# One fixed order for all engines: a list schedule in the kernel in place of key-sorted stages with visits

## The chip, the core and the metric

The kernel runs on one core of one Trainium2 chip. Five engines work at the same time, each through its own queue of instructions: PE (TensorE, matmuls; its weight loads are a row of their own, PEld), DVE (VectorE), ACT (ScalarE), POOL (GpSimd), and SP (SyncE), which here only issues DMA transfers. They meet through semaphores. The metric is the device time of one execution in microseconds (us); 374.27 us before, the median of three runs.

## The reference, cut to what matters

A gated linear attention feeds a feed-forward layer with a convolution along the sequence. There are 4 sequences of 768 steps, 8 heads of 48, so d_model is 384; d_ff is 1024.

```python
f = 1.0 / (1.0 + np.exp(-f_logit))
for t in range(S):
    state = f[:, :, t, :, None] * state + np.einsum('bhd,bhe->bhde', k[:, :, t], v[:, :, t])
    y[:, :, t] = np.einsum('bhd,bhde->bhe', q[:, :, t], state)
...
h = np.maximum(x @ w_in, 0.0)                 # x: y with heads side by side
hp = np.concatenate([zeros, h, zeros], axis=1)
for k in range(3):
    conv_out += conv_w[k][None, None, :] * hp[:, k:k + S, :]
gate = 1.0 / (1.0 + np.exp(-conv_out))
return (h * gate @ w_out).astype(np.float32)
```

The three weight arrays come as float64, q, k, v and f_logit as float32.

## The kernel before, in words

**Tiling.** The sequence is cut into chunks of 128 steps: 6 per sequence, 24 in all, numbered n. Three chunks make half a sequence, a unit u; there are 8 units. Attention goes chunk by chunk, the feed-forward unit by unit. All of it is unrolled; nothing loops on the chip.

**Attention of a chunk.** *Gate*: two activations (Exp, Ln) turn f_logit (tile fb) into log decays; from group 3 on, three chunks at once and split into two reduced-precision parts (cgh, cgl). *Stage a*: a matmul with a triangle sums the decays into pl; ACT takes two exponentials, fi and fd; k is multiplied by fi, q by fd; the last row of fd is the chunk's decay, fetched by small matmuls into pl (L223) for the first chunks and by small DMAs (L238, L246) later. *Stage b*: four transposes each of k and q (ptk, ptq, L254), copied to kT and qT (L256). *Scores*: 16 matmuls into pa (L298), copied under a causal mask into am (L300). *Values*: py gets the old state times q (L340), then v times am (L346); ACT and DVE split it into two parts of xT (L356, L357). *State*: 16 matmuls of k with v (L313) and two DVE steps (L322, L323) give the next state. pa, py and fi have one buffer, am, kT and qT two, xT three, k four, q three. After each third chunk six DMAs inside the core gather part of xT (L362).

**Weights.** w_in comes in six tiles, w_out in eight. `split_f64` (L98) turns the two 32-bit words of each number into a high and a low float part: three ACT and up to seven DVE steps, and for tiles marked d or a in `CFG["ez"]` three matmuls on PE (pzwi, pzwo) that form the low part, copied out by DVE or ACT. The raw words lie in the buffers of g and xT for that time.

**Feed-forward.** `mm1` (L367) takes two of the eight d_ff tiles of a unit: nine matmuls each into ph (L385), Relu into hb (L388), the three taps of the convolution on ACT and DVE (L390, L396, L397), a Tanh (L399) and the gate product (L400) into g. `mm2` (L402) takes 128 steps: g is split into gh and gl (L415, L416), 24 matmuls go into po (L422), ACT copies to ob, SP stores. ph, po and the weight joins share two PSUM banks.

**What sets the order.** Each stage is put into a list with a key (L440 to L475), mostly a chunk number with an offset from CFG; the list is sorted by key and traced. What each engine then runs is not this order: the framework orders the instructions again by priority and its own timeline (`schedule_with_timeline_sim=True`, L614). `visit` (L272) ties parts of it down: from chunk 8 (`ng`) on, score, value and state matmuls get a high priority (`hp`); the first value matmul of a chunk waits for the copies of kT, qT and am of this and the next chunk; the state matmuls follow the last visited PE instruction. Two matmuls on zeros (L264) go ahead of all. Behind the list, a count checks the decays (L483 to L489) and a branch leads to a slow path that is not taken here.

Of the kernel before, what the change touches and what calls it, by code (L numbers as in the profile page):

```python
# [9 lines left out]
F32 = mybir.dt.float32  # L10
# [12 lines left out]
CFG = dict(ez="ddddddaaaavvvv", ng=8, hp=4000, tb=2, groups=[3, 3, 3, 3, 3, 3, 3, 3], sg=3, f1=2.6, g1=2.6, gv=9, gl=5.2, g=3.9, l=3.2, a=1.8, b=0.8, s=0.2, v=0.5, wil=(-2.3, -1.1), wis=(-0.7, 0.9), cw=1.3, wol=(1.3, 1.0), wos=2.1, wo=0.35, m1=0.5, m1s=0.9, m2=1.5, m2s=1.2, ek=(12, 24), ec='d', er='p', tp=0, tf=2, nw=2, gd=0, q0=2, lf=3, kpool=2, eg='d', eq='d', es='d', em='d', ew='p', xb=3, nf=6, fe='a', kb=4, qb=3, vb=4, lv=2.2, cb=1, sb=3, fi=1)  # L23

@with_exitstack
def gla_moe_kernel(ctx, tc, q_in, k_in, v_in, f_in, w_in, conv_w, w_out, out):
# [5 lines left out]
    q, k, v, f_logit = [t.rearrange("b s h d -> b h s d")[:, :, :, :D] for t in (q_in, k_in, v_in, f_in)]  # L32
# [7 lines left out]
    GC = max(groups)  # L40
    first = [sum(groups[:g]) for g in range(len(groups) + 1)]
# [12 lines left out]
    ld = fast.enter_context(tc.tile_pool(name="ld", bufs=2))  # L54
    wk = fast.enter_context(tc.tile_pool(name="wk", bufs=2))
# [21 lines left out]
    def zeroed(shape, n, name, eng):  # L77
        ts = [wk.tile(shape, F32, name=f"{name}{i}", bufs=1) for i in range(n)]
        for t in ts:
            eng.memset(t, 0.0)  # L80
        return ts

    kp_b = [wk.tile([P, H, HP], F32, name=f"kp{i}", bufs=1) for i in range(CFG["kb"])]
    qp_b = [wk.tile([P, H, HP], F32, name=f"qp{i}", bufs=1) for i in range(CFG["qb"])]
    a_b = zeroed([P, 2, NP, P], 2, "am", nc.vector)
    s_b = [wk.tile([P, NP * D + GAP], F32, name=f"st{i}", bufs=1) for i in range(2)]
# [4 lines left out]

# [6 lines left out]
    def split_f64(raw, n, hi, lo, nm, tile=0):  # L98

        pr = raw.rearrange("p (n w) -> p n w", w=2)  # L100
        lw, hw = pr[:, :, 0], pr[:, :, 1]
        r = raw.shape[0]
        ms = wk.tile([P, 2, WC], I32, tag="gl", name=f"ms{nm}")
        m, s = ms[:r, 0, :n], ms[:r, 1, :n]
        mf, sf = m.bitcast(F32), s.bitcast(F32)
        nc.scalar.activation(mf, hw.bitcast(F32), AF.Abs)
# [23 lines left out]
    raws = {}  # L130

    def raw_in(kt, i):
        if kt == 0 and ("i", i) not in raws:
            raws["i", i] = wk.tile([P, KT, 2 * WC], I32, tag="g32", name=f"wis{i}")
        return raws["i", i][:, kt]

    def raw_out(f):
        i = f // 4
        if ("o", i) not in raws:
            raws["o", i] = (wk.tile([P, 4, 2 * DM], I32, tag="g32", name=f"wos{i}") if i == 0 else  # L140
                            wk.tile([P, 4, 2 * DM], I32, tag="xT", name=f"wos{i}", bufs=CFG["xb"]))
        return raws["o", i][:, f % 4]

    def load_w_in(kt, i):
        nc.sync.dma_start(raw_in(kt, i), w_in[kt * P:(kt + 1) * P, i * WC:(i + 1) * WC].bitcast(I32))
# [473 lines left out]
```

## Time and profile before

| what | before |
|---|---|
| median of three runs | 374.27 us (371.98 to 374.36) |
| the profiled execution | 374.75 us |
| its span, first to last instruction | 373.0 us |
| mean granted TensorE clock | 0.969 |
| busy PE / PEld | 349.7 / 308.4 us |
| busy DVE / ACT / POOL | 266.0 / 236.6 / 15.0 us |
| instructions | 7517 |
| read from HBM / written | 28.37 / 4.75 MB |

Busy times are of one engine and overlap with the others. The ends of matmuls are modelled, so a busy PE need not be PE at its peak. A row of the timeline has start and length in us, engine, line, operation, output<-inputs, and in brackets the idle time before it with what ended it; neighbouring rows of one kind are merged (x3), and rows of one engine overlap a little where instructions are pipelined. A row of the chain of waits has start, length, and what the end of the kernel waited for. A row of a group has line, engine, operation, count, then busy us and mean ns of one. SPq is SP's queue, which issues transfers; PEldq is PE's queue.

### The profile page before, as it was taken

The numbers are of one execution on the slowest core, as the hardware profiler recorded it, in microseconds if no ns is written. First come the engines' busy times: TensorE is split into PE (matmuls) and PEld (weight loads), VectorE is DVE, ScalarE is ACT, GpSimd is POOL, SyncE is SP. The second block draws the span as 40 slices with busy tenths as digits, with TensorE's granted clock in tenths as the row PEclk, the third lists the DMA queues.
The fourth block names the chain that finished last, engine by engine and source line by source line (L and its number), as shares of the span: only waits on it lengthen the run. The fifth ranks groups of instructions, "written<-read, shape, count | busy, mean of one in ns | idle before, by whom it ended". The sixth has DMA issues, their size and how long they took to land.

```text
span 373.0 us, 7517 instructions
## 1 busy us (share of the span) xinstructions
PE 349.7 (94%) x2927; PEld 308.4 (83%) x2927; DVE 266.0 (71%) x443; ACT 236.6 (63%) x425; POOL 15.0 (4%) x45
## 2 busy tenths in 40 slices
PE   4788999977999998999999999999999999999993
PEld 1456677865899986899999898999999999999992
DVE  3598897989577836867768887679578766576620
ACT  3769887896957657756947664476455744566530
POOL 1110000014000000100000000000000000000000
PEclk9598999998799999999999999999999999999998
DMA  7998226324312360233321442223021000201011
GB/s 229 357 354 320 103 44 188 114 79 119 106 29 72 93 195 15 100 69 98 101 73 51 112 126 67 66 71 101 22 72 34 21 2 24 54 23 42 21 46 50
DMA packets 28854, 36.05 MB, mean 97 GB/s; under 512 B 10847, under 2 KB 20106, under 8 KB 28810
## 3 DMA queue, kind: packets, MB, share of 16 engines
q1 hardware_dynamic: 28810, 35.49, 31.3%
q8 instruction: 25, 0.41, 0.4%
q14 instruction: 19, 0.16, 0.1%
HBM read 28.37 MB, written 4.75 MB: 89 GB/s over the span
## 4 chain that ended last, share of the span: by engine, by line
PE 75%; DVE 10%; ACT 6%; DMA 4%; issue 3%; SPq 1%; ACTq 0%; DVEq 0%
PE po L422 26%; PE ph L385 23%; PE py L346 6%; PE pa L298 5%; PE py L340 3%; PE ptk L254 3%; PE py L313 2%; PE ptq L254 2%; DMA fb<-in_f_logit_dram 2%; PE pl L214 2%; DMA wis<-in_moe_w_in_dram 2%; DVE g L397 1%; PE pzwi L125 1%; ACT fb L188 1%; DVE g L396 1%
## 5 line engine op out<-in xcount | busy, mean ns | idle before, releaser
L385 PE MATMUL ph<-xT,wi 128*128 128x384 f32 x576 | 113.3, 345 | 0.8 <-ACT ob L425 0.8
L385 PEld LDWEIGHTS ph<-xT,wi 128*128 128x128 f32 x576 | 99.8, 189 | 4.5 <-issue 1.4
L422 PE MATMUL po<-wo,gh 128*128 128x384 f32 x384 | 99.8, 339 | 1.5 <-ACT hb L388 1.5
L422 PEld LDWEIGHTS po<-wo,gh 128*128 128x128 f32 x384 | 69.2, 188 | 2.7 <-ACT hb L388 1.8
L422 PE MATMUL po<-wo,gl 128*128 128x384 f32 x192 | 65.3, 340 | 0.0
L396 DVE SCALAR_TENSOR_TENSOR g<-hb,cw,g 128x384 f32<-128x384 f32 (+1 forms) x64 | 39.3, 616 | 19.8 <-ACT g L390 19.3
L388 ACT ACTIVATE hb<-ph 128x384 f32<-128x384 f32 x64 | 31.5, 492 | 30.6 <-PE ph L385 30.4
L415 ACT CAST gh<-g 128x1024 fp32r<-128x1024 f32 (+4 forms) x34 | 26.7, 803 | 27.1 <-PE po L422 21.9
L416 DVE TENSOR_TENSOR gl<-g,gh 128x1024 fp32r<-128x1024 f32 (+4 forms) x34 | 30.5, 909 | 17.9 <-ACT gh L415 15.9
L399 ACT ACTIVATE g<-g 128x768 f32<-128x768 f32 (+1 forms) x32 | 27.1, 846 | 25.1 <-DVE g L397 25.1
L400 DVE SCALAR_TENSOR_TENSOR g<-g,hb 128x768 f32<-128x768 f32 (+1 forms) x32 | 30.7, 960 | 15.4 <-ACT g L399 15.2
L397 DVE SCALAR_TENSOR_TENSOR g<-hb,cw,g 128x384 f32<-128x384 f32 (+1 forms) x64 | 39.5, 619 | 2.5
L390 ACT ACTIVATE g<-hb,cw 128x384 f32<-128x384 f32 (+1 forms) x64 | 39.6, 620 | 1.9
L422 PEld LDWEIGHTS po<-wo,gl 128*128 128x128 f32 x192 | 36.0, 188 | 0.8 <-issue 0.5
L300 DVE COPY_PREDICATED am<-mask,pa 128x1024 f32<-128x1024 uint8 x24 | 31.7, 1320 | 1.1 <-PE pa L298 1.1
L346 PE MATMUL py<-am,v 128*48 128x128 f32 (+1 forms) x384 | 28.9, 291 | 2.9 <-DVE xT L357 1.7
L298 PE MATMUL pa<-qT,kT 48*128 48x128 f32 x384 | 29.9, 286 | 1.6 <-ACT qT L256 1.1
L298 PEld LDWEIGHTS pa<-qT,kT 48*128 48x128 f32 x384 | 24.3, 187 | 6.9 <-issue 1.8
L346 PEld LDWEIGHTS py<-am,v 128*48 128x48 f32 (+1 forms) x384 | 22.2, 136 | 8.6 <-issue 4.6
L357 DVE TENSOR_TENSOR xT<-py,xT 112x512 fp32r<-112x512 f32 x24 | 16.5, 689 | 4.2 <-ACT xT L356 4.2
L356 ACT CAST xT<-py 112x512 fp32r<-112x512 f32 x24 | 14.0, 584 | 7.8 <-PE py L346 7.8
L378 POOL COPY hb<-hb 128x4 f32<-128x4 f32 x16 | 9.9, 619 | 186.1 <-DVE g L400 186.1
(106 smaller groups left out, 400.5 us busy)
## 6 DMA issues: line engine op xcount, KB each, us to landing
kp<-in_k_dram SPq DMA_DIRECT2D x24, 256.0 KB
qp<-in_q_dram SPq DMA_DIRECT2D x24, 256.0 KB
fb<-in_f_logit_dram SPq DMA_DIRECT2D x24, 192.0 KB
v<-in_v_dram SPq DMA_DIRECT2D x24, 192.0 KB
out_dram<-ob SPq DMA_DIRECT2D x24, 192.0 KB
wis<-in_moe_w_in_dram SPq DMA_DIRECT2D x6, 512.0 KB
wos<-in_moe_w_out_dram SPq DMA_DIRECT2D x8, 384.0 KB
xT<-xT SPq DMA_DIRECT2D x48, 48.0 KB
```

The source lines that it names most:

```text
L298: nc.tensor.matmul(pa[:, j, p, :], kT[r, p, :], qT[r, p, :], start=True, stop=True)
L300: ready.setdefault(n, []).append(nc.vector.copy_predicated(am, mask, pa).ins)
L346: nc.tensor.matmul(py[HP * o:HP * o + w, j, p // 2, :], lhs, am[:, j, p, :], start=c == 0 and p < 2, stop=(p >= 2))
L385: nc.tensor.matmul(ph, wi[:, t, wl, f * P:(f + 1) * P], xts[b, hf][:, t, xl, :], start=(i == 0), stop=(i == 3 * KT - 1))
L388: nc.scalar.activation(hb[:, 2:HS + 2], ph, AF.Relu, scale=0.5)
L390: nc.scalar.activation(cv, hb[:, 1:n + 1], AF.Copy, scale=cw[:, 1, f:f + 1])
L396: nc.vector.scalar_tensor_tensor(cv, hb[:, 2:n + 2], cw[:, 2, f:f + 1], cv, ALU.mult, ALU.add)
L397: nc.vector.scalar_tensor_tensor(cv, hb[:, 0:n], cw[:, 0, f:f + 1], cv, ALU.mult, ALU.add)
L399: nc.scalar.activation(cv, cv, AF.Tanh)
L400: nc.vector.scalar_tensor_tensor(cv, cv, 1.0, h_b[:, fp:fp + 2, 1:n + 1], ALU.add, ALU.mult)
L416: nc.vector.tensor_tensor(lo, g[:, f:f + k], hi.bitcast(F32), ALU.subtract)
L422: nc.tensor.matmul(po, g[:, f, :], wo[:, f, wl, :], start=(i == 0), stop=(i == 3 * NF - 1))
```

## The change

The keyed stages, `visit` and the helper functions go. Every step becomes an item (`Op`) of a `Plan`: which engine, how many ns, what to issue, a key, which items it needs (`need`), which buffer it takes from a ring (`take`) and which buffers it uses (`use`). An item is about one ACT, DVE or POOL instruction or DMA, or one group of matmuls: the transposes of k, those of q, the 16 scores, the carry (old state times q), the 16 values, the state matmuls, nine ph matmuls, sixteen po matmuls on gh and eight on gl, the three joins of a weight tile.

`Plan.order()` is a list schedule, run in Python while the kernel is built. It keeps a clock. Whenever an engine is free, it takes, of the items whose needs are done and whose buffers are free, the one with the smallest key; rings hand out buffers in the order of keys. An item ends after its ns, and is seen by others after a further latency for its engine. From matmuls of the r kind (reduced precision) to the f kind 95 ns are added, for an ACT table change 1283. A load lands by a pipe that moves 340 bytes per ns, 1500 ns after its issue at the earliest, plus 700; at most eight are in flight. `trace()` then issues all items in the order of planned starts under `manual_schedule()`, so that this is the order on each engine.

Keys are a chunk number with new offsets from CFG: per unit for mm1 and mm2 (`m1`, `m2`), per weight tile for the splits (`w1s`, `w2s`). Further edits in it:

- Weight loads of the first half of w_in have the key -5.73, conv_w -5.15, f of chunk n n - 3.97 (n + 27.31 from group 3 on), k and q n - 1.96, v n + 10.34.
- Copies to kT and qT, and the last copy of a weight split, go to ACT or DVE, whichever the plan has free first.
- 11 weight tiles are joined on PE and 3 on DVE (before 10 and 4).
- The first two k products move from POOL to DVE. The two warm-up matmuls on zeros are gone. The state needs no tmp tile.
- mm2's matmuls go first over gh, then over gl, where before each tile of d_ff took both. The last 128 steps are no longer split into quarters.
- The count of decays is traced behind the whole plan.

The arithmetic, the matmuls' shapes and the number of buffers of each kind stay; the raw weight words may now lie in two of xT's buffers and in both of g's, whichever is free first.

```diff
+    LAT = dict(PE=210, ACT=70, DVE=70, POOL=100, SP=60)
...
+            for e in free:
+                if free[e] > now + 1e-6:
+                    continue
+                if e == "SP" and len(dma) >= 8 and dma[-8] > now + 1e-6:
+                    continue
+                for o in sorted(ready[e], key=lambda o: o.key):
...
+                    for r, i in o.take:
+                        if fifo[r][head[r]] is not o:
+                            ok = False
+                            break
+                        b = next((b for b in self.rings[r] if not (b[1] & taken)), None)
...
+                ns = o.engs[e]
+                if e == "PE":
+                    if mode == "r" and o.mode == "f":
+                        ns += 95
+                    mode = o.mode
...
+                o.start, o.on, o.end = now, e, now + ns
+                free[e] = o.end
+                seen = o.end + self.LAT[e]
+                if e == "SP":
+                    pipe = max(o.end + 1500, pipe) + o.size / 0.34
+                    seen = pipe + 700
...
+        return sorted(done, key=lambda o: (o.start, o.key))
...
+        o = plan.op("PE", 1092, score, (n, "sc"), need=copies, use=[KT_, QT_], take=[("A", ("A", n))], mode="f")
+        o = plan.op("DVE", 1320, lambda e, n=n, AM=AM: nc.vector.copy_predicated(buf(AM), mask, buf(("A", n))), (n, "sc"),
+                    need=[o], use=[("A", n)], take=[("am", AM)])
...
+        oc = plan.op("PE", 590, carry, kv, need=[stated[n - 1]] + copies, use=[QT_], take=[("Y", Y)], mode="f") if c else None
+        ov = plan.op("PE", 1024, value, kv, need=[o, oc, ld_v], use=[V, AM] + ([Y] if c else []),
+                     take=[] if c else [("Y", Y)], mode="f")
...
+            o = plan.op("PE", 595, rank, ks, need=[ov, ok_], use=[K, V, Y], mode="f")
...
+                    o = pl.op("PE", 1575, mm1, key, need=list(x_ready[u]) + (W_IN[f // (NF // 2)] if extra else []), use=[("xT", u)],
+                              take=[("mm", ph)], mode="r")
...
+                o = pl.op("PE", 2820, mm2, key, need=his + (W_OUT if extra else []), use=[gh], take=[("mm", po)], mode="r")
+                o = pl.op("PE", 1410, lambda e, mm2=mm2: mm2(e, z=1), key, need=[o] + los, use=[gl, po], mode="r")
...
+    moe(plan, gathered, [1])
+    with tc.manual_schedule():
+        plan.trace()
...
-    pw = ps.tile([P, NP * P], F32, tag="mm", name="pw", bufs=2)
-    zr = a_b[0][:, 0].rearrange("p n t -> p (n t)")
-    for i in range(CFG["nw"]):
-        nc.tensor.matmul(pw, zr[:, :P], zr, start=True, stop=True)
...
-        with tc.high_priority(offset=CFG["hp"]) if whole else ExitStack():
-            yield
...
-        if part == 0:
-            for i in ready[n] + ready.get(n + 1, []):
-                tc.add_manual_dep(mine[0], i.name, DATA, reason="visit")
-        else:
-            tc.add_manual_dep(mine[0], last_pe[0].name, NOSYNC, reason="visit")
```

More of the change, by code (lines that the diff above doesn't have):

```diff
@@ L1 @@
-from contextlib import ExitStack, contextmanager
+import heapq
+from itertools import count
+from contextlib import ExitStack
 import numpy as np
@@ L75, in gla_moe_kernel, with sb, bank @@
     mask = mask1.rearrange("p (j n t) -> p j n t", j=1, n=1).broadcast_to([P, 2, NP, P])
[L77 to L86, printed above, removed]
+    def sb(shape, name, pool=None, dtype=F32):
+        return (pool or wk).tile(shape, dtype, name=name, bufs=1)
+    def bank(t):
+        return t.rearrange("p (n t) -> p n t", t=P)
+    plan, serial = Plan(), count()
+    am_b = [sb([P, 2, NP, P], f"am{i}") for i in range(2)]
+    for t in am_b:
+        nc.vector.memset(t, 0.0)
+    s_b = [sb([P, NP * D + GAP], f"st{i}") for i in range(2)]
     for t in s_b:
@@ L130, in gla_moe_kernel @@
[L130 to L142, printed above, removed]
@@ new lines, in load_raw @@
+    def load_raw(raw, at, src, r, key, nbytes, take):
+        i = ("raw", raw)
+        n = src.shape[-1]
+        return plan.op("SP", 430, lambda e: nc.sync.dma_start(plan.buf(i)[:r, at:at + n], src), key,
+                       take=[("raw", i)] if take else [], use=[] if take else [i], size=nbytes)
+    W_IN, W_OUT = [[None] * KT for _ in range(DFF // WC)], [None] * NF
+    for i in range(DFF // WC):
+        for kt in range(KT):
+            cs = slice(i * WC, (i + 1) * WC)
+            o = load_raw(("wi", i), kt * RW, w_in[kt * P:(kt + 1) * P, cs].bitcast(I32), P, (0.01 * kt, "w1", i), 512, kt == 0)
+            W_IN[i][kt] = split_f64(("wi", i), kt * RW, P, WC, (0, "w1s", KT * i + kt), o, lambda kt=kt, cs=cs: wi[:, kt, 0, cs],
+                                    lambda kt=kt, cs=cs: wi[:, kt, 1, cs], f"wi{kt}_{i}", CFG["ez"][KT * i + kt])
@@ L171, in gla_moe_kernel @@
+    N = len(steps)
     group_of = [g for g, m in enumerate(groups) for _ in range(m)]
[L172 to L197 removed]
@@ new lines, in out_of, with carry, value @@
+        def out_of(Y, p, j, w):
+            return buf(Y)[HP * side(p, j):HP * side(p, j) + w, j, p // 2, :]
+        def carry(e, n=n, Y=Y, QT_=QT_):
+            for p, j in heads:
+                r = slice(HP * j, HP * j + D)
+                w = HP if side(p, j) == 0 else D
+                nc.tensor.matmul(out_of(Y, p, j, w), s_b[n % 2][r, p * D:p * D + w], buf(QT_)[r, p, :], start=(p < 2),
+                                 stop=False)
+        def value(e, c=c, Y=Y, V=V, AM=AM):
+            for p, j in heads:
+                h = 2 * p + j
+                w = HP if side(p, j) == 0 else D
+                nc.tensor.matmul(out_of(Y, p, j, w), buf(V).rearrange("p h d -> p (h d)")[:, h * D:h * D + w],
+                                 buf(AM)[:, j, p, :], start=c == 0 and p < 2, stop=(p >= 2))
@@ L452, in gla_moe_kernel @@
-    for n in range(N):
-        plan(n - CFG["l"], lambda n=n: load_kq(n))
-        plan(n - CFG["lv"], lambda n=n: load_v(n))
-        plan(n - CFG["a"], lambda n=n: stage_a(n))
-        plan(n - CFG["b"], lambda n=n: stage_b(n))
-        plan(n - 1.2, lambda n=n: decay_out(n))
-        plan(n - 0.7, lambda n=n: decay_in(n))
-        plan(n - 1 + CFG["v"] + 0.02 if n > CFG["ng"] else n, lambda n=n: scores(n))
-        plan(n + CFG["v"] + 0.01, lambda n=n: state(n))
-        plan(n + CFG["v"], lambda n=n: values(n))
```

726 lines of the change are left out of this document (414 added, 312 removed).

## The prediction

> **What bounds the kernel now.** I read the busy table first, then the table of four stretches, then the early stretches alone, the chain of waits, and single rows of the timeline.
>
> ```profile
> PE 349.7 (94%) x2927; PEld 308.4 (83%) x2927; DVE 266.0 (71%) x443; ACT 236.6 (63%) x425; POOL 15.0 (4%) x45
> ```
>
> ```profile
> 0.00:100.00 100.00, 85.50 (x731) 62.41 (x731) 80.26 (x163) 76.67 (x152) 9.88 (x21) 0.90 0.57 183
> 100.00:160.00 60.00, 57.40 (x496) 51.90 (x494) 43.23 (x68) 39.83 (x69) 2.38 (x7) 1.00 0.31 86
> 160.00:340.00 180.00, 180.00 (x1553) 167.62 (x1552) 130.28 (x193) 107.11 (x180) 2.73 (x17) 1.00 0.22 63
> 340.00:373.00 33.00, 26.79 (x155) 26.43 (x153) 12.24 (x21) 12.97 (x26) 0.00 (x0) 0.96 0.11 39
> ```
>
> The columns of the second are stretch, length, busy time of PE, PEld, DVE, ACT, POOL, granted clock, DMA share, GB/s. PE at 94% would leave 23 us. But from 160 to 340 us PE never stops, and PEld, its weight loads, stands at 167.62 of 180, 93%. In the first 100 us PE reads 85.50 and PEld only 62.41: there the matmul spans are stretched (cold clock, single matmuls), and less work is done than the PE column says. I take the full stretch as the yardstick: 180 / 167.62 = 1.074 us of PE time for each us of weight load. The whole kernel then holds 308.36 x 1.074 = 331.1 us of PE work. The first stretch did 67.0 us of it in 100 (33.0 lost), the second 55.7 in 60 (4.3 lost), the last 28.4 in 33 (4.6 lost). That makes up the 373.0. [...]
>
> So a new order can win nothing from 160 us on. It can win at the start: 33.0 + 4.3 us. Since both times are for one profiled execution, the sum is made against its 374.75 us (span 373.0, 1.75 around it), 0.1% above the median of 374.27.
>
> ```profile
> 0.00:20.00 20.00, 12.60 (x52) 6.94 (x54) 9.74 (x22) 9.94 (x19) 2.84 (x16) 0.74 0.88 299
> 40.00:60.00 20.00, 19.57 (x206) 13.59 (x202) 18.75 (x46) 15.52 (x39) 0.00 (x0) 1.00 0.39 116
> 20.00:100.00 80.00, 72.89 (x684) 55.47 (x681) 70.52 (x142) 66.73 (x133) 7.04 (x5) 0.94 0.49 154
> 91.00 1.97 PE L346 MATMUL py<-am,v 128*48 128x128 f32 x16 [1.71 <-DVE xT L357]
> ```
>
> What starves PE there is mainly DVE: 70.52 of 80 us, its fullest 20 us 18.75. In the full stretch 130.28 us of DVE feed 180 us of PE, so a us of DVE is worth 1.38 us of PE, and DVE runs 28% idle later. ACT's 66.73 is close behind. The last row is the seventh chunk's values: by 91 us seven of 24 chunks are through.
>
> **The change, part by part.**
>
> *No waiting for a fixed neighbour (gain).* The list schedule gives each engine, whenever it is free, the first item by key whose inputs and buffers are there by the planned clock. DVE's idle time from 20 to 100 us is 80 - 70.52 = 9.48 us; all of it removed is worth 13.1 us of PE. If DVE reaches only its best share (18.75 / 20, 75.0 of 80), it is 4.5 x 1.38 = 6.2. I take 11, nearer the upper end: the best share itself is that of the old order, and spans of neighbouring instructions overlap.
>
> *Weights loaded first (gain).*
>
> ```profile
> 0.81 0.40 SPq L202 DMA_DIRECT2D kp<-in_k_dram  x1
> 2.20 1.38 SPq L145 DMA_DIRECT2D wis<-in_moe_w_in_dram  x3
> 7.09 0.66 ACT L106 ACTIVATE mswi<-wis 128x512 f32<-128x512 f32 x1 [0.90 <-DMA wis<-in_moe_w_in_dram]
> 9.72 0.66 ACT L106 ACTIVATE mswi<-wis 128x512 f32<-128x512 f32 x1 [1.98 <-DMA wis<-in_moe_w_in_dram]
> 10.80 0.48 ACT L218 ACTIVATE fi<-pl 128x384 f32<-128x384 f32 x1
> 6.28 0.88 PE L214 MATMUL pl<-fb,tri 128*128 128x384 f32 x2 [0.79 <-ACT fb L189]
> ```
>
> By the new keys SP issues w_in's first half (-5.73), conv_w, three chunks of f, then k and q. Before, 0.70 MB (k, q, f) went ahead of w_in; at 299 GB/s that is 2.4 us, so DVE starts its splits up to 2.4 us earlier, worth 3.3 us of PE. Chunk 0's f moves back by 1.5 MB against 0.5 MB, 3.4 us, but ACT now sits between 7.09 and 10.80 behind w_in's rows before it takes fi, so chunk 0 loses nothing or little. From 0 to 3.3; I take 2.
>
> *Attention ahead of the feed-forward (gain).*
>
> ```profile
> 325.15 6.26 PE ph L385 x36
> 346.00 20.81 PE po L422 x120
> L300 DVE COPY_PREDICATED am<-mask,pa 128x1024 f32<-128x1024 uint8 x24 | 31.7, 1320 | 1.1 <-PE pa L298 1.1
> L357 DVE TENSOR_TENSOR xT<-py,xT 112x512 fp32r<-112x512 f32 x24 | 16.5, 689 | 4.2 <-ACT xT L356 4.2
> L232 DVE TENSOR_TENSOR qp<-qp,fd 128x384 f32<-128x384 f32 x24 | 14.1, 588 | 0.0
> L231 DVE TENSOR_TENSOR kp<-kp,fi 128x384 f32<-128x384 f32 x22 | 12.2, 556 | 3.9 <-ACT fi L218 3.7
> L322 DVE TENSOR_TENSOR stmp<-py,st 112x192 f32<-112x192 f32 x16 | 5.6, 351 | 8.4 <-PE py L313 8.4
> L323 DVE TENSOR_TENSOR st<-stmp,ft_all 112x192 f32<-112x192 f32 x16 | 5.6, 353 | 0.1
> L396 DVE SCALAR_TENSOR_TENSOR g<-hb,cw,g 128x384 f32<-128x384 f32 (+1 forms) x64 | 39.3, 616 | 19.8 <-ACT g L390 19.3
> L397 DVE SCALAR_TENSOR_TENSOR g<-hb,cw,g 128x384 f32<-128x384 f32 (+1 forms) x64 | 39.5, 619 | 2.5
> L400 DVE SCALAR_TENSOR_TENSOR g<-g,hb 128x768 f32<-128x768 f32 (+1 forms) x32 | 30.7, 960 | 15.4 <-ACT g L399 15.2
> 20.00:100.00 80.00, 3.65 (x8) 1.19 (x8) 20.56 (x48) 12.44 (x24) 0.94 0.49 154
> ```
>
> The last row counts the instructions on mswo alone, the w_out splits: 20.56 us of DVE before 100 us. A ph matmul takes 6.26 / 36 = 0.174 us, a po one 20.81 / 120 = 0.173; 576 of each are 100.2 and 99.9, and leave 131.0 us of PE, 5.5 per chunk of attention with the weight joins in it. A chunk costs DVE 1.32 + 0.69 + 0.59 + 0.56 + 0.35 + 0.35 = 3.86 us, so 1.42 us of PE per us; a ph item gives 1.57 for 0.62 + 0.62 + 0.48 = 1.71, so 0.92. In the old keys the first ph item (3.5) stood level with the values of chunk 3 (n + 0.5); in the new (3.54 against n - 1.89) with chunk 5.4, and the w_out splits move back by about as much. 2.4 more chunks first are 9.3 us of DVE at 0.50 more, 4.6 us; in place of w_out splits, which DVE can do in its later idle time, up to 2.4 x 5.5 = 13.2. Buffers (three of xT, one bank each for scores and values) may forbid it: 0. I take 6.
>
> *The stretch from 100 to 160 (gain).*
>
> ```profile
> 130.58 0.86 SPq L179 DMA_DIRECT2D fb<-in_f_logit_dram  x2
> 131.54 0.38 SPq L426 DMA_DIRECT2D out_dram<-ob  x1
> 132.93 4.07 DMA fb<-in_f_logit_dram
> 142.06 0.62 PE L422 MATMUL po<-wo,gh 128*128 128x384 f32 x2 [1.52 <-ACT hb L388]
> ```
>
> The third load of an f tile follows the other two only behind an out store on SP (third row, from the chain: 132.93 to 137.00), its gates wait, and PE's stop comes after them. The new f loads have the lowest urgency on SP, but a tile that is free with nothing else ready is filled at once, and a store enters SP's order only where its copy is planned to be done. 0 to 4.3; I take 3.
>
> *Costs.*
>
> ```profile
> 125.65 0.51 PE L422 MATMUL po<-wo,gh 128*128 128x384 f32 x2
> 126.09 0.67 PE L313 MATMUL py<-v,kp 128*64 128x48 f32 x16
> 126.69 1.16 PE L298 MATMUL pa<-qT,kT 48*128 48x128 f32 x16
> 366.88 0.48 ACT L425 COPY ob<-po 128x384 f32<-128x384 f32 x1 [3.67 <-PE po L422]
> L486 PE MATMUL pcnt<-ones,oks x2: 163/164/164, 307.9 to 308.0; 128*1 128x1 f32 x2
> L489 PEldq TENSOR_LOAD <-cnt_i x1: 487/487/487, 363.5 to 363.5; - x1
> L491 PEldq COMPARE_BRANCH  x1: 3585/3585/3585, 364.1 to 364.1; - x1
> ```
>
> Without visits state and scores need not follow each other. Two po take 0.44 us to the next start instead of 0.347: each turn from po or ph to attention costs 0.09. If all six PE items of a chunk stand alone instead of in two groups, 24 x 4 x 0.09 = 8.6; some will meet anyway: I take 2 (0 to 8.6). The count for the slow path (L486) ran at 308 us and PE's branch of 3.59 us began at 364.1, before its last matmul ended at 366.8. Traced behind the list, it comes last on PE: 0.16 + the load 0.49 + 3.59 = 4.2 us and the semaphore steps, beside the last store's 0.48 and landing (span end 373.0). I take 0.8 (0 to 2). The warm-up matmuls go: the clock of the first 20 us, 0.74 even with them, falls; PE's work there is 6.94 x 1.074 = 7.5 us, and at worst half of it takes as long again; but DVE and the loads end last there. I take 0.5 (0 to 3.7). [...] One w_out tile more is joined on PE, two kp products go from POOL to DVE, both within DVE's regained time: 0.2.
>
> Sum: 11 + 2 + 6 + 3 - 3.5 = 18.5, so 374.75 - 18.5 = 356 us. Ends: 6.2 of gain and no cost gives 368.5. The best is the floor: no PE work before 6.28, where the first f has let pl start, 331.1 of work, 6.2 after the last matmul: 343.6 + 1.75 = 345. Own range 345 to 368.
>
> **The rivals.** *Planned arrivals come early.* The plan moves loads at 340 GB/s; the first 20 us ran at 299. The 12 MB that 40 us carry at that rate are planned for 35.2, 4.8 us of lateness, and behind a late item everything on DVE and ACT waits. Mechanism: DVE keeps the lower 6.2, loses the 2 of the start and 4.8 x 1.38 = 6.6; with 6 + 3 and the costs that leaves about 5: 370 us. For it: ACT's two stops on w_in above. Against: the old order was fixed as well and filled 18.75 of 20. [...] Chance 0.12, half of it within 1%.
>
> *Bare waits in the steady part: slower.* Visits tied score and value matmuls to their copies; now each attention item is placed by planned latencies. If one step per chunk comes late by the mask copy's 1.32 us, PE, now without a stop for 180 us, loses 24 x 1.32 = 31.7; less 18.5 that is 388 us. It decides from 18.5 / 24 = 0.77 us per chunk. Against: the plan's lengths are the rows' (1320 for the mask copy, 960 for the gate). For: they are fixed, and 28% idle DVE is all the slack. Chance 0.12.
>
> *Nothing moves.* Dependences alone set the early order, and 375 us remains. The old early stops show engines idle while others had work, against it. 0.04.
>
> **How the numbers follow.** Forecast 0.72, all of it more than 1% faster; 1% is about what a measurement here can tell from no change. Faster 0.72 + 0.06 = 0.78, within 1% 0.06 + 0.04 = 0.10, slower 0.12. The range 345 to 370 holds the forecast and half of the first rival, 0.78.
>
> **What would show it.** Right: PEld in the first 100 us well over 62.41 (about 75 to 80), DVE over 73 between 20 and 100, stretches after 160 as full as before, last matmul near 348. Start term: a w_in row on ACT before 5.5 us. Attention term: the seventh chunk's values well before 91 us. Tail: the count beside the last matmul, and more than 6.2 us behind it. Wrong: PE stops of over 0.5 us per chunk after 160 (second rival), DVE or ACT waiting on loads in the first 40 us for more than 5 us (first).

## The result, and the profile after

The changed kernel takes 359.31 us (median of four runs, 358.22 to 359.56), beside 374.14 us before (four runs, 371.98 to 374.36): a ratio of 0.9611 with a 95% interval of 0.957 to 0.9651. The profiled execution took 358.22 us, with a span of 356.5 us and a mean granted clock of 0.999. Where a run of some kernel lies over 1.5% above the fastest of the same kernel, the ratios below leave it out (two runs of the first experiment, one of the old kernel with attention ahead, one beside the run with less PE work). The forecast was 356 us, with a range of 345 to 370.

The page of the changed kernel, its busy table and its chain by engine:

```profile
PE 336.6 (94%) x2927; PEld 302.2 (85%) x2927; DVE 257.2 (72%) x431; ACT 240.2 (67%) x428; POOL 9.6 (3%) x43
```

```profile
PE 91%; ACT 4%; DMA 2%; DVE 1%; issue 0%; SPq 0%; ACTq 0%
```

The same chain before:

```profile
PE 75%; DVE 10%; ACT 6%; DMA 4%; issue 3%; SPq 1%; ACTq 0%; DVEq 0%
```

PE stands at 94% as before, so the busy share alone shows nothing. The chain shows it: 91% of what the end waited for is now PE. Before, it was 75%, with DVE at 10%.

The stretches of the changed kernel, columns as in the prediction (stretch, length, busy PE, PEld, DVE, ACT, POOL, clock, DMA share, GB/s):

```profile
0.00:20.00 20.00, 8.00 (x46) 4.62 (x48) 12.34 (x29) 11.38 (x23) 1.43 (x15) 1.00 0.90 301
0.00:100.00 100.00, 86.29 (x887) 66.64 (x888) 82.49 (x167) 77.52 (x158) 3.68 (x19) 1.00 0.63 202
100.00:160.00 60.00, 60.00 (x503) 56.05 (x503) 50.75 (x79) 49.55 (x80) 1.88 (x8) 1.00 0.33 92
160.00:340.00 180.00, 179.47 (x1480) 169.07 (x1479) 121.55 (x184) 110.61 (x186) 4.06 (x16) 1.00 0.19 53
340.00:357.00 17.00, 10.80 (x62) 10.48 (x60) 2.45 (x2) 2.52 (x5) 0.00 (x0) 0.96 0.15 52
20.00:100.00 80.00, 78.29 (x845) 62.01 (x844) 70.15 (x139) 66.14 (x136) 2.25 (x4) 1.00 0.56 178
```

In the first 100 us PE ran 887 matmuls instead of 731. From 20 to 100 us it is busy for 78.29 us instead of 72.89, and DVE, which the prediction took for the bound, is as full as before (70.15 against 70.52); only in the first 20 us does it do more (12.34 against 9.74). From 100 to 160 us PE does not stop.

The gain can be split without any yardstick. Each row below runs from the first real matmul to the start of the last copy out of PSUM, first of the kernel before, then of the changed one:

```profile
6.28:366.88 360.60, 346.26 (x2923) 307.16 (x2923) 263.61 (x435) 233.78 (x422) 13.55 (x30) 0.97 0.32 96
```

```profile
11.19:350.88 339.69, 336.55 (x2927) 302.20 (x2927) 251.42 (x416) 234.62 (x420) 8.18 (x28) 1.00 0.32 96
```

PE starts 4.91 us later. Its idle time falls from 360.60 - 346.26 = 14.34 to 339.69 - 336.55 = 3.14, which is 11.20 less. Its own busy time falls by 9.71, and the tail by 0.50 (373.0 - 366.88 = 6.12 against 356.5 - 350.88 = 5.62). The sum is 4.91 - 11.20 - 9.71 - 0.50 = -16.5, the whole difference of the spans. The 9.71 was not in the prediction: the matmuls ran shorter, although there are four more of them (one weight tile more is joined on PE). A good part of it, by the estimate below, is the clock, which was low behind the old order's stops (0.58 from 11.70 to 20 us, 0.50 from 91 to 96). Stretches and single rows of the kernel before, the last ones around the stop that the prediction quoted at 91 us:

```profile
11.70:20.00 8.30, 8.29 (x46) 5.46 (x48) 5.22 (x10) 4.97 (x11) 1.06 (x1) 0.58 1.02 353
20.00:40.00 20.00, 17.69 (x169) 12.03 (x166) 18.18 (x38) 16.57 (x39) 1.00 (x1) 0.91 0.83 301
80.00:100.00 20.00, 16.70 (x153) 13.75 (x151) 16.65 (x29) 16.24 (x26) 5.60 (x3) 0.83 0.36 97
88.00:91.00 3.00, 1.16 (x17) 1.00 (x17) 3.00 (x6) 1.17 (x3) 1.45 (x1) 0.89 0.81 242
91.00:94.00 3.00, 3.00 (x21) 2.67 (x22) 2.99 (x5) 1.94 (x4) 0.00 (x0) 0.50 0.29 45
94.00:96.00 2.00, 2.00 (x10) 2.00 (x9) 0.63 (x1) 1.99 (x2) 0.19 (x1) 0.50 0.45 82
```

```profile
84.08 0.63 PE L254 MATMUL ptk<-ident,kp 128*128 128x128 f32 x4 [1.10 <-issue]
85.70 1.09 PE L346 MATMUL py<-am,v 128*48 128x128 f32 x16
88.12 1.16 PE L298 MATMUL pa<-qT,kT 48*128 48x128 f32 x16 [0.49 <-DVE am L300]
92.90 1.12 PE L254 MATMUL ptk<-ident,kp 128*128 128x128 f32 x4
```

From 88 to 91 us PE was busy for 1.16 of 3 us, with no single wait over 1.71, and then the granted clock was 0.50 for five us: the same sixteen value matmuls took 1.97 us instead of 1.09, the same four transposes 1.12 instead of 0.63. If the low clock is put down to the wait ahead of it, which no run tests alone, this wait is paid twice, 1.71 us of standing and, as an estimate, 2.5 us (5 x 0.50) of slow work behind it. If busy time is lost in proportion to what the clock column lacks to 1, the old kernel lost some 3.5 us up to 20 us (8.29 x 0.42), 1.6 from 20 to 40 (17.69 x 0.09) and 2.8 from 80 to 100 (16.70 x 0.17). That is 7.9 us, an estimate, against 1.6 in the changed kernel's slow start, which its column does not show (the last section, and the run with nine matmuls on zeros): some 6.3 of the 9.71.

Single rows of the changed kernel's timeline answer the prediction's signs:

```profile
6.98 1.22 ACT L283 ACTIVATE gx<-xT 128x512 f32<-128x512 f32 x2 [4.88 <-DMA xT<-in_moe_w_in_dram]
9.13 0.51 ACT L370 ACTIVATE fb<-fb 128x384 f32<-128x384 f32 x1
11.19 1.62 PE L405 MATMUL ss<-fb,tri 128*128 128x384 f32 x2 [11.19 <-ACT fb L372]
14.52 0.39 PE L314 MATMUL mm<-ob,idr 128*128 128x512 f32 x1
18.54 0.81 PE L405 MATMUL ss<-fb,tri 128*128 128x384 f32 x2
65.46 1.09 PE L480 MATMUL Y<-am,v 128*48 128x128 f32 x16
68.27 2.01 PE L552 MATMUL mm<-xT,wi 128*128 128x384 f32 x10
350.88 0.48 ACT L614 COPY ob<-mm 128x384 f32<-128x384 f32 x1 [0.92 <-PE mm L608]
```

The seventh chunk's values start at 65.46 us instead of 91.00. The first feed-forward matmul stands behind them, at 68.27. The last matmul ends at 350.88 - 0.92 = 349.96 us, where about 348 was forecast.

### The profile page after: what moved, and what is told of

Its sections match the earlier page's. It is cut to its first block, busy times and chain, and to the rows that moved or that the text cites. A ratio compares the mean times of both kernels' runs of the same rounds, so it can differ in the third digit from the quotient of the medians.

```text
span 356.5 us, 7515 instructions
## 1 busy us (share of the span) xinstructions
PE 336.6 (94%) x2927; PEld 302.2 (85%) x2927; DVE 257.2 (72%) x431; ACT 240.2 (67%) x428; POOL 9.6 (3%) x43
## 4 chain that ended last, share of the span: by engine, by line
PE 91%; ACT 4%; DMA 2%; DVE 1%; issue 0%; SPq 0%; ACTq 0%
PE mm L552 29%; PE mm L608 29%; PE Y L480 7%; PE A L458 7%; PE ss L447 6%; PE Y L502 3%; PE Y L473 3%; PE mm L312 2%; PE ss L405 2%; DMA xT<-in_moe_w_in_dram 2%; PE ss L403 2%; ACT xT L490 1%; PE mm L314 1%; PE mm L313 1%; PE ss L418 1%; ACT gx L289 0%
## 5 line engine op out<-in xcount | busy, mean ns | idle before, releaser
L552 PE MATMUL mm<-xT,wi 128*128 128x384 f32 x576 | 108.2, 341 | 0.0
L608 PE MATMUL mm<-wo,gx 128*128 128x384 f32 x576 | 105.6, 340 | 0.0
L608 PEld LDWEIGHTS mm<-wo,gx 128*128 128x128 f32 x576 | 101.3, 188 | 0.7 <-issue 0.5
L552 PEld LDWEIGHTS mm<-xT,wi 128*128 128x128 f32 x576 | 99.4, 188 | 1.4 <-issue 0.7
L599 DVE TENSOR_TENSOR gx<-g,gx 128x1024 fp32r<-128x1024 f32 (+2 forms) x28 | 29.6, 1073 | 28.7 <-PE mm L608 28.4
L562 ACT ACTIVATE hb<-mm 128x384 f32<-128x384 f32 x64 | 31.2, 492 | 25.8 <-PE mm L552 25.4
L595 ACT CAST gx<-g 128x1024 fp32r<-128x1024 f32 (+2 forms) x28 | 26.0, 938 | 24.4 <-PE mm L608 20.0
L461 DVE COPY_PREDICATED am<-mask,A 128x1024 f32<-128x1024 uint8 x24 | 31.5, 1314 | 5.1 <-PE A L458 4.6
L458 PE MATMUL A<-qT,kT 48*128 48x128 f32 x384 | 27.9, 285 | 0.4 <-ACT qT L450 0.4
L480 PE MATMUL Y<-am,v 128*48 128x128 f32 (+1 forms) x384 | 26.3, 278 | 0.0
L480 PEld LDWEIGHTS Y<-am,v 128*48 128x48 f32 (+1 forms) x384 | 20.5, 129 | 4.8 <-issue 1.7
L490 ACT CAST xT<-Y 112x512 fp32r<-112x512 f32 x24 | 14.0, 584 | 15.4 <-PE Y L480 8.8
```

Of the source, the lines that this page charges most:

```text
L458: nc.tensor.matmul(buf(("A", n))[:, j, p, :], buf(KT_)[r, p, :], buf(QT_)[r, p, :], start=True, stop=True)
L461: o = plan.op("DVE", 1320, lambda e, n=n, AM=AM: nc.vector.copy_predicated(buf(AM), mask, buf(("A", n))), (n, "sc"), need=[o], use=[("A", ...
L480: nc.tensor.matmul(out_of(Y, p, j, w), buf(V).rearrange("p h d -> p (h d)")[:, h * D:h * D + w], buf(AM)[:, j, p, :], start=c == 0 and p < ...
L552: nc.tensor.matmul(buf(ph)[:, :HS], wi[:, t, wl, f * P:(f + 1) * P], x_view(pl, u)[:, t, xl, :], start=(i == 0), stop=(i == 3 * KT - 1))
L562: nc.scalar.activation(hb[:, 2:HS + 2], buf(ph)[:, :HS], AF.Relu, scale=0.5)
L599: los.append(pl.op("DVE", 150 + 134 * nn * NF // 128, lambda e, hv=hv, lv=lv, src=src: nc.vector.tensor_tensor(lv(), src(), hv().bitcast(F ...
```

## The experiments

Where "the changed kernel" is named, its 359.31 us is meant. Runs of one group shared the runs of the kernel before, whose medians were 372.49 to 373.60, and 374.14 beside the changed kernel: a difference of about 1 us between groups is not read. What the plan's clock gives is the planned end of the last matmul, which the plan tells while the kernel is built: 345.06 us for the changed kernel.

### The fixed order alone undone

```diff
-    with tc.manual_schedule():
-        plan.trace()
+    plan.trace()
```

> The changed kernel with the same items, keys, lengths and trace order, but without the manual schedule around the trace, so that the framework may order the instructions again by its own timeline. Theory A (the order that the list schedule planned is itself the gain): the time goes back a good part of the way to 374, to 364 to 374, and the gaps in the first 160 us return. Rival B (splitting the work into items and the new keys carry the gain, whoever sorts them): 357 to 361, as the changed kernel's 359.3.

Measured: 375.82 us, ratio 1.0063 (1.0028 to 1.0097). All of the gain is gone (375.44 us is the median without the two runs left out), although items, keys, loads and the plan's order of tracing are those of the changed kernel; the framework's own scheduler orders them again. PE's waits (line and tile, releaser, us, times, longest), a stretch, and the split from the first matmul to the last copy in this kernel:

```profile
PE mm L312 <- DVE gx L290: 12.2, 2, 10.6
PE ss L447 <- ACT kT L450: 2.5, 2, 1.8
PE mm L608 <- ACT hb L562: 2.1, 1, 2.1
```

```profile
20.00:100.00 80.00, 71.14 (x739) 54.98 (x738) 66.86 (x134) 64.31 (x128) 2.34 (x3) 0.98 0.50 159
10.61:367.60 356.99, 345.40 (x2927) 305.07 (x2927) 252.07 (x417) 232.70 (x419) 14.71 (x28) 1.00 0.30 92
```

From 20 to 100 us PE is busy for 71.14 us, less than the 72.89 of the kernel before. The 10.6 us in the first wait are the time up to PE's first matmul. Behind it the two parts of the gain come back in near equal size: idle time is 356.99 - 345.40 = 11.59, which is 8.45 more than in the changed kernel, and the same 2927 matmuls are busy 345.40 - 336.55 = 8.85 longer. The clock explains only a part of the second (0.91 from 20 to 40 us); the rest was not settled. The rest of the change, without the order, gives nothing.

### The order kept, the lengths wrong

```diff
+        engs = {e: 600 if e in ("ACT", "DVE") else x for e, x in engs.items()}
```

> Every ACT and DVE item is planned at 600 ns instead of its measured length (PE, POOL and SP lengths stay). Only the planned order changes, not the work. Theory A (measured lengths matter, since an order planned with wrong ones makes in-order engines wait): 363 to 372, with new PE stops in the first 160 us. Rival B (data dependences and keys set the order, lengths little): 357 to 361.

Measured: 381.91 us, ratio 1.0238 (1.0184 to 1.0291), outside the expectation on the slow side. A fixed order planned with wrong lengths is worse than no fixed order. The stretches and waits of this kernel:

```profile
100.00:160.00 60.00, 54.86 (x472) 49.84 (x471) 50.29 (x83) 51.71 (x85) 3.00 (x9) 0.97 0.27 74
160.00:340.00 180.00, 173.74 (x1460) 162.48 (x1458) 116.86 (x174) 101.98 (x172) 7.07 (x16) 0.99 0.22 60
```

```profile
PE ss L406 <- ACT kT L451: 3.2, 2, 2.5
PE Y L503 <- ACT xT L491: 2.9, 1, 2.9
PE Y L503 <- DVE xT L493: 2.1, 3, 1.3
PE A L459 <- ACT qT L451: 1.9, 1, 1.9
```

PE stops on copies of attention, also after 160 us (173.74 of 180 busy, where the kernels before and after read 180.00 and 179.47). That is the mechanism of the prediction's second rival, and in this plan the measured lengths keep it out. The plan's choice between ACT and DVE is made anew with these lengths too; its share was not taken apart.

### Feed-forward moved 2.4 chunks forward again

```diff
-           w2s=(2.26, 1.43, 1.57, 4.78, -0.47, 5.05, 6.16, 5.87),
-           m1=(0.54, 0.16, -1.41, -0.09, 0.1, 1.45, 1.44, 5.48), m1d=0.58,
+           w2s=(-0.14, -0.97, -0.83, 2.38, -2.87, 2.65, 3.76, 3.47),
+           m1=(-1.86, 0.16, -1.41, -0.09, 0.1, 1.45, 1.44, 5.48), m1d=0.58,
```

> The keys of the first unit's ph items and of all w_out splits are 2.4 smaller, which sets them level with attention as they were before the change. The prediction's attention term (6, between 0 and 13.2) says: 364 to 372. If running attention ahead is worth nothing, because DVE has the same work to do in either order: 357 to 361.

Measured: 364.82 us, ratio 0.9759 (0.9708 to 0.981), so 5.5 us of the gain hang on it. The plan's clock gives the same: 350.55, 5.5 later. In this kernel's stretch

```profile
20.00:100.00 80.00, 75.55 (x767) 59.38 (x765) 66.43 (x136) 67.60 (x137) 3.05 (x4) 0.96 0.50 160
```

PE is 2.74 us less busy than in the changed kernel, and the clock column shows 0.96 instead of 1.00.

### Less DVE work

Three of the five DVE steps of each w_out split are left out, for all eight tiles.

```diff
-        o = step("DVE", 170 + 250 * x, lambda e: V.tensor_scalar(
+        o = o if light else step("DVE", 170 + 250 * x, lambda e: V.tensor_scalar(
...
-        m = step("DVE", 150 + 530 * x, lambda e: V.scalar_tensor_tensor(
+        m = o if light else step("DVE", 150 + 530 * x, lambda e: V.scalar_tensor_tensor(
```

> Leaves out three of the five DVE steps of every w_out split (about 1.27 us each, 10.2 us of DVE before 70 us; w_out is wrong). Theory A (the early part is still bound by DVE, a us of DVE worth 1.38 us of PE, as the prediction had it): up to 14 us less, 345 to 352. Rival B (with the new order PE is fed without a break from its first matmul on, and DVE work has cover): 357 to 360.

Measured: 359.42 us, ratio 0.9617 (0.9569 to 0.9665): nothing. In the stretch

```profile
20.00:100.00 80.00, 77.66 (x848) 61.53 (x847) 70.19 (x130) 68.84 (x139) 2.04 (x4) 1.00 0.55 172
```

DVE stays at 70.19, so other work stands in the room that was made, and PE gets no more done; over the whole kernel DVE's busy time falls from 257.2 to 252.0 us. DVE's time is not what bounds the changed kernel. Whether it bounded the kernel before, as the prediction says, no run here tests.

### Less PE work

For half of the outputs one matmul on gl is run instead of eight.

```diff
...
+                    light = z == 1 and b in (1, 2)
-                    i = 16 * z
-                    for f in range(NF):
+                    i = 16 * z + (NF - 1) * light
+                    for f in range((NF - 1) * light, NF):
```

> Of the eight matmuls on gl for each 128 steps, seven are left out for 12 of the 24 outputs (sequences 1 and 2), so that those outputs are wrong; the plan, its lengths and its order stay. 84 matmuls go, at 105.6 / 576 = 0.183 us each 15.4 us of PE, all of it between 150 us and 300 us. Theory A (PE's own work is the length of the changed kernel from 11 us on): nearly all of it comes back, 344 to 346 us, in contrast to the DVE steps that were left out, of which nothing came back. Theory B (ACT, DVE or the fixed order stand right behind PE): half or less comes back, 352 or more.

Measured: 350.83 us, ratio 0.9392 (0.9353 to 0.9432), 8.5 us less than the changed kernel. That lies between the two theories. Of the 15.4 us of PE, more than half comes back, where the DVE steps left out gave nothing; but the next wait is near. This kernel from its first matmul to its last copy, and PE's waits:

```profile
10.76:343.41 332.65, 324.31 (x2843) 287.63 (x2843) 250.07 (x416) 233.52 (x419) 8.23 (x28) 1.00 0.33 98
```

```profile
PE mm L609 <- ACT ob L615: 2.8, 2, 1.6
PE mm L552 <- ACT ob L615: 1.2, 1, 1.2
```

PE now waits 4.0 us for a PSUM bank whose copy stands in ACT's fixed order behind other items; the plan still had the long matmuls in it. The split tells where the rest of the 15.4 went: PE's busy time fell by 336.55 - 324.31 = 12.24 only, so the estimate of 0.183 us for a matmul was too high, and idle time rose from 3.14 to 332.65 - 324.31 = 8.34, which is 5.20, most of it these waits. With a start 0.43 us earlier, that gives the 7.5 us between the two profiled spans.

### Matmuls on zeros ahead of the plan

```diff
+        zr = am_b[0][:, 0].rearrange("p n t -> p (n t)")
+        for _ in range(18):
+            nc.tensor.matmul(ps_s[0], zr[:, :P], zr, start=True, stop=True)
```

> Eighteen matmuls of 128 by 384 on zeros go to PE ahead of the plan; nothing else changes. In the changed kernel PE starts at 11.19 us and its first score matmuls take 1.62 us for two where later ones take 0.81, until about 14.3 us. Theory A (the slow first matmuls delay everything that follows, since PE is full from then on): two or three us of half-rate work come back at full rate, 357 to 358 us, and the first two transposes and scores take 0.8 instead of 1.6. Theory B (the first 20 us wait for weights and gates anyway): 359, unchanged.

Measured: 365.28 us, ratio 0.98 (0.9749 to 0.985). This says nothing for or against the theories, since the edit was mis-sized: eighteen of these (512 columns wide, not 384) took 17.56 us and put the first real matmul at 19.45 us. It measured something else: with PE starting 8.26 us later, the end came 6.0 us later. Half as many, then:

```diff
-        for _ in range(18):
+        for _ in range(9):
```

> Nine matmuls of 128 by 512 on zeros instead of the eighteen of the run before, which took 17.56 us and put the first real matmul at 19.45 us; nine should take about 8.8 us and end near 10.9 us, just ahead of the first real matmul at 11.19. Theory A (the first 3 us of real work run at half rate, and PE is full behind them): the first two score sums take 0.81 instead of 1.62 us, and 2 to 2.6 us come back, 357 us. Theory B (cold matmuls cost nothing that the waits of the first 20 us do not cost anyway): 359, unchanged.

Measured: 359.04 us, ratio 0.963 (0.9597 to 0.9663), the same. The rows of this kernel:

```profile
2.06 10.50 PE L623 MATMUL ss<-am 128*128 128x512 f32 x18 [2.06 <-DVE am L225]
12.40 0.81 PE L405 MATMUL ss<-fb,tri 128*128 128x384 f32 x2
18.16 0.81 PE L405 MATMUL ss<-fb,tri 128*128 128x384 f32 x2
```

The zeros themselves began slowly (the nine more of the run before added 17.56 - 10.50 = 7.06 us) and took 10.50 us instead of the 8.8 expected, so the real work starts 1.21 us later. (These rows are sums of decays under the triangle; the expectations call them score sums.) From the first to the second such sum it takes 18.16 - 12.40 = 5.76 us, against 18.54 - 11.19 = 7.35 in the changed kernel. Over this piece of work the slow start costs 1.59 us, then, and the later start of the real work took 1.21 of it away again. That the first real work runs slow, as Theory A says, is shown; that it delays the end is not, since the remaining 0.38 us is less than the spread of these runs (358.29 to 359.67).

### The first gates loaded ahead of the weights

```diff
-           v=10.34, a=-4.58, ft=16.82, b=-3.72, sc=-2.87, va=-1.89, st=-5.42, ga=-13.17, w1=(-5.73, -0.65),
-           w1s=(-10.73, -13.33, -10.47, -7.85, -5.72, -3.4), cw=-5.15, w2=(9.54, 2.63),
+           v=10.34, a=-4.58, ft=16.82, b=-3.72, sc=-2.87, va=-1.89, st=-5.42, ga=-13.17, w1=(-3.9, -0.65),
+           w1s=(-10.73, -13.33, -10.47, -7.85, -5.72, -3.4), cw=-1.5, w2=(9.54, 2.63),
```

> The first half of w_in is loaded at key -3.9 instead of -5.73 and conv_w at -1.5 instead of -5.15, so the first gates' inputs go ahead of the weight words, as in the kernel before. PE then begins near 5.2 us instead of 11.2 us. Theory A (the later start of PE in the changed kernel is a loss, since PE is full behind it): up to 3 us faster, 356 to 358. Theory B (weights first pays: without them the early stretch has too little PE work that is ready): by the plan's own clock the last matmul ends 3.5 us later, 363. The prediction's term for weights first was 2 us of gain.

Measured: 362.37 us, ratio 0.9717 (0.9667 to 0.9766), 3.1 us slower than the changed kernel; the plan's clock had said 3.5. The rows of this kernel show why an early start of PE is not a gain by itself:

```profile
4.51 1.62 PE L405 MATMUL ss<-fb,tri 128*128 128x384 f32 x2 [4.51 <-ACT fb L372]
7.09 0.80 PE L418 MATMUL ss<-ident,fd 32*48 32x1 f32 x16 [0.96 <-ACT fd L412]
12.60 1.09 PE L447 MATMUL ss<-ident,k 128*128 128x128 f32 x4 [4.71 <-ACT wi L299]
```

PE starts 6.68 us earlier, does 2.4 us of work, and waits 4.71 us for the weight splits. DVE is busy for 10.34 us of the first 20, against 12.34 in the changed kernel. The other keys were not chosen again for this order, so it prices the two edits within this plan, not the idea in general.

### The old kernel with attention ahead

```diff
-wos=2.1, wo=0.35, m1=0.5, m1s=0.9, m2=1.5, m2s=1.2,
+wos=4.5, wo=0.35, m1=2.9, m1s=0.9, m2=2.5, m2s=1.2,
```

> The kernel before, with later keys for the feed-forward alone (m1 0.5 to 2.9, m2 1.5 to 2.5, w_out splits 2.1 to 4.5), so that attention is some 2.4 chunks ahead as in the changed kernel. Theory A (attention ahead is worth its 5.5 us under any scheduler): 368 to 369 us beside 374. Theory B (the gain needs the fixed order, since here the keys only set priorities): 372 to 376, unchanged. Above 376 the framework's order fills PE worse with feed-forward held back.

Measured: 385.62 us, ratio 1.0369 (1.0286 to 1.0453). A like shift is worth 5.5 us in the fixed order and costs some 11 to 13 in the old one; it is not the same one, since here mm1 moves in all units, not in the first alone, and mm2 moves by 1.0 (383.77 us is the median without the run left out, beside 372.49). The stretches:

```profile
20.00:100.00 80.00, 70.77 (x716) 54.19 (x717) 71.08 (x144) 69.18 (x139) 3.69 (x5) 0.96 0.51 158
160.00:340.00 180.00, 172.59 (x1454) 161.08 (x1454) 122.96 (x184) 101.22 (x169) 3.76 (x19) 0.99 0.20 55
```

PE gets less done early, not more, and is no longer full after 160 us. Other shifts were not tried.

### Engines fixed by hand

The copies to kT and qT all go to ACT, the last copy of a weight split to DVE.

```diff
-        return plan.op(dict(ACT=140 + 480 * x, DVE=150 + 530 * x), 0,
+        return plan.op(dict(DVE=150 + 530 * x), 0,
...
-            copies.append(plan.op(dict(ACT=580, DVE=685), 0, lambda e, dst=dst, pt=pt: (
+            copies.append(plan.op(dict(ACT=580), 0, lambda e, dst=dst, pt=pt: (
```

> The copies to kT and qT all go to ACT and the last copy of each weight split all to DVE, instead of to whichever of the two the plan has free first; the order is planned again with this. Theory A (the list schedule's choice of the engine is part of the gain): by the plan's own clock the last matmul ends 5.2 us later, 363 to 366 us. Theory B (DVE and ACT have room, so the choice gives nothing): 359 to 360.

Measured: 365.44 us, ratio 0.9793 (0.9738 to 0.9849): 6.1 us slower, where the plan's clock said 5.2.

### Better keys by the plan's clock

All offsets of CFG are replaced by others, among them these:

```diff
-f=(-3.97, 27.31), gate=(-3.17, 3.04), kq=-1.96,
+f=(-4.99, 26.32), gate=(-0.12, 20.37), kq=-3.68,
...
-m1=(0.54, 0.16, -1.41, -0.09, 0.1, 1.45, 1.44, 5.48), m1d=0.58,
+m1=(-0.7, 0.21, -1.34, 1.69, -0.92, 1.3, 1.87, 7.74), m1d=0.15,
...
-        for src, dst, o, tag, ns in ((K, KT_, ok_, "kT", 435), (Q, QT_, oq_, "qT", 355)):
+        for src, dst, o, tag, ns in ((K, KT_, ok_, "kT", 540), (Q, QT_, oq_, "qT", 355)):
```

> The same items and the same list schedule, with other keys: the offsets in CFG found by a search over the plan's own clock, after the length of the k transposes was put at 540 ns (the chip's pitch) instead of 435. The plan's last matmul then ends at 344.9 us; with the old keys and 540 ns it ends at 350.4. Theory A (differences of the plan's clock come out on the chip, as they did with the gates first, 3.5 us planned and 3.1 measured, and with fixed engines, 5.2 and 6.1; old order run through at 540 ns ends at 346.9, so 2.0 us are to be had): 357 to 358 us. Theory B (the plan's clock is not good to 1%: its last few us are fitted to lengths that the chip does not keep): 359 or slower.

Measured: 359.35 us, ratio 0.9638 (0.9604 to 0.9671). Theory B: no gain. From its first real matmul to its last copy this kernel shows

```profile
10.79:351.49 340.70, 338.81 (x2927) 303.53 (x2927) 252.96 (x417) 236.11 (x419) 7.67 (x28) 1.00 0.32 96
```

The plan did what it was searched for: idle time falls from 3.14 to 340.70 - 338.81 = 1.89, and PE starts 0.40 earlier. But the busy time of the same 2927 matmuls is 2.26 us longer, and that takes it back. The plan gives a group of matmuls one length wherever it stands (but for the 95 ns of a mode change), and the chip does not. The largest rise is in the transposes (28.07 to 29.49 us); which neighbours cause it was not settled. With the zeros as well:

> Both edits, the new keys and the nine matmuls on zeros. Theory A (both gains stand and add up, 2 and 2 to 2.6 us): 355 us. Theory B (one of them is none): 357. Theory C (neither): 359 or slower.

Measured: 358.88 us, ratio 0.9619 (0.9586 to 0.9653). It lies 0.4 us below the changed kernel, less than the spread of its own runs (357.38 to 359.53): no version here is shown to beat it.

## Why the prediction was right, and where it was not

The forecast was 3.3 us too low. Its direction holds, and so does the place of the gain: PE's stops in the first 160 us are nearly gone. What the forecast had wrong is how the gain comes about (through more DVE work early), so that its total is better than its terms.

**The yardstick (failed).** The step took 1.074 us of PE for each us of weight load, and forecast PEld of 75 to 80 in the first 100 us. It reads 66.64, although 156 more matmuls ran. Between first real matmul and last copy, PEld fell from 307.16 to 302.20 with four matmuls more, so the old sum was partly slow loads: at a clock of 0.50 it reads 2.00 of 2.00 us (94 to 96 us), denser than the 93% (167.62 of 180) of the stretch that the step took as its yardstick. And the work moved forward is attention, which loads less per us of PE than the feed-forward: by the page 20.5 us of PEld beside 26.3 of PE for the values (L480), against 101.3 beside 105.6 for L608. The floor of 331.1 us of PE work was not far off all the same: the changed kernel's PE is busy for 336.55.

**No waiting for a fixed neighbour, 11.** The order is the term on which all else hangs: undone, the whole gain goes (some 16 us, 375.44 against 359.31). But the way was wrong. DVE was to rise over 73 us between 20 and 100 and each us of it was to be worth 1.38 us of PE. DVE stayed at 70.15, and leaving DVE work out of the changed kernel gave nothing. What changed must then be which work DVE did when; that is inferred, no run varies it alone. The gain came out at PE itself: 11.20 us less idle time, and shorter matmuls. That 11.20 is near the 11 of this term is chance, since it holds the idle time that the terms for attention and for 100 to 160 us were to save as well.

**Weights loaded first, 2 (right in size, not as reasoned).** A row of w_in on ACT was to stand before 5.5 us. It stands at 6.98, against 7.09 before. Three loads of 512 KB were issued within 1.35 us, and by the profile's page they land a median of 6.6 us after issue. So the first split gained 0.1 us, not 2.4. But the second tile was there as well: its row follows at once in the changed kernel (x2 in the row at 6.98) and stood at 9.72 before. DVE did 12.34 - 9.74 = 2.60 us more work in the first 20 us, near the 2.4 that the term counts on. What was wrong is "chunk 0 loses nothing or little": the first gate on ACT moved from 5.11 to 9.13 us, and PE's first matmul from 6.28 to 11.19. Within this plan the early weights are worth 3.1 us all the same (the gate-first run), because PE's early start found nothing to go on with there.

**Attention ahead, 6.** The run that moved feed-forward forward again lost 5.5 us. The reason given, a us of DVE that brings more PE work in attention, is not shown by it, and the old kernel, given a like shift, lost some 11 to 13. The term is shown only inside the fixed order.

**The stretch from 100 to 160, 3.** PE went from 57.40 to 60.00 of 60, which is 2.6 us. The stop on hb is gone. The reason given is not shown: in the changed kernel, too, SP issues a third load of f only behind an out store (at 128.21 and 127.31 us).

**Costs.** Turns between r and f matmuls were put at a cost of 2. Counted in the two timelines there are some 70 before and some 43 after, so about 27 x 0.09 = 2.4 us, an estimate, were a gain: attention items met more often without visits, not less. The tail count was to run last on PE (0.8). It did not; the rows of the changed kernel for the count and for the branch:

```profile
L630 PE MATMUL ss<-ones,oks x2: 163/164/164, 259.2 to 259.2; 128*1 128x1 f32 x2
```

```profile
L635 PEldq COMPARE_BRANCH  x1: 3402/3402/3402, 348.1 to 348.1; - x1
```

It stands outside the fixed part and the framework moved it up to 259 us. The tail is 5.62, not over 6.2. The warm-up's absence was put at a cost of 0.5 (0 to 3.7); that at worst half of the early work takes as long again was an estimate. The changed kernel's first decay sum did take 1.62 us instead of 0.81, and its slow start costs 1.59, but the kernel before, with its warm-up and a wait of 4.54 us behind the first gate, ran at a clock of 0.58 from 11.70 to 20 us, an estimated 3.5. So no cost against the kernel before is shown.

**What was missed.** The clock. The prediction read 0.90 in the first 100 us as part of the lost time but never asked what would become of it once PE stood less (it reads 1.00 in the changed kernel). By the estimate above that was worth some 6.3 us, and the 4.91 us of later start, which it did not see either, stand against it. With the 2.4 us of fewer turns, about 1 us of the 9.71 is left without a cause, by these estimates.

**The terms do not add.** Undone one by one, the order costs some 16 us, the lengths 22.6, the engines 6.1, attention 5.5, the early weights 3.1: together over three times the gain. So these prices overlap and cannot be added. For attention ahead, the old kernel speaks against a price that holds without the rest, though its shift was a wider one; for the others this was not tested. That the prediction's sum of parts came near owes something to luck: a gain and a cost that it missed (some 6.3 and 4.91) are of similar size.

**The rivals.** Planned arrivals early (370): the plan's starts of the 24 score groups, set 0.81 us later for the span's start, are met 0.3 to 2.0 us late up to 150 us, 4.2 late at the last, and PE's named waits after its first matmul are these of the changed kernel:

```profile
PE ss L405 <- ACT kT L450: 1.2, 2, 0.6
PE ss L447 <- DVE kT L450: 0.8, 1, 0.8
PE A L458 <- ACT qT L450: 0.4, 1, 0.4
PE Y L502 <- DVE xT L492: 0.3, 1, 0.3
```

That is 2.7 us, none of it on a load. On ACT one wait for a load stands in the first 40 us, the 4.88 us before the row at 6.98, and on DVE none; the sign for this rival was more than 5 us. Bare waits in the steady part (388): 0.53 us of idle PE in 180, not 0.77 per chunk; with wrong lengths the rival came (381.91).

## What to carry to other kernels

When several engines feed one, the order on all of them is one object: plan it with measured lengths, fix it, and do not take the price of a single piece of it (a key, a load, a choice of engine) as its worth alone or under another scheduler: the one piece that was tried in both, attention ahead (by a wider shift in the old kernel), gained 5.5 us in one and lost over 11 in the other. The plan's own clock told steps of 3 to 6 us well (5.5 planned and 5.5 measured, 3.5 and 3.1, 5.2 and 6.1), but not the last 2. Price a PE stall by its length and, where the clock column shows them, by the slow matmuls behind it (1.71 us and an estimated 2.5 at 91 us in the old kernel), and test a supposed bound by leaving out some of its work: 84 PE matmuls gave 8.5 us, 24 DVE steps none.

## What the runs showed of the hardware

- The granted clock fell to 0.50 for five us behind a stretch in which PE was busy for 1.16 of 3 us and no wait was longer than 1.71 us.
- The clock column can miss a slow start. The changed kernel's first decay sum took 1.62 us where later ones take 0.81, and the row at 14.52 is the first at full speed (0.39 us, as the same step at 15.84), 3.3 us behind the first matmul, while the column reads 1.00 for 0 to 20 us.
- Issuing loads first hardly landed the first of them sooner, but the second: with three loads of 512 KB issued at once, ahead of all else, ACT took the first at 6.98 us and was done with both at 8.20; with 0.70 MB of others ahead of them it took them at 7.09 and 9.72.
- The old kernel's clock read 0.58 from 11.70 to 20 us, behind a wait of PE of 4.54 us.
